# Attention on one core: products with the values in two runs a pair, last 64 rows and keys by full 128x128 transposes

## The chip, the core and the metric

The kernel runs on one core of a Trainium2 chip. The metric is the device time of one execution in microseconds (us). Engines are named as in the profile: PE is TensorE (matmuls), PEld its weight loads, DVE is VectorE, ACT is ScalarE, POOL is GpSimd, SP issues most of the DMAs.

## What is computed

The reference is an attention with a relative position bias, then a mixture of experts, then a maximum of three products. Only the attention is touched by the change (cut to what matters):

```python
B, H, S, D = 4, 8, 576, 64
scores = scale * q @ k.T                 # per batch and head, 576 x 576
scores = scores + bias                   # one 576 x 576 table per head
attn = exp(scores - max(scores))
attn = attn / (sum(attn) + 1e-9)
x = attn @ v                             # per batch and head, 576 x 64
```

576 is four times 128 and a rest of 64 rows (the tail), both of queries and of keys.

## The kernel before, in words

Heads are taken two at a time: there are 16 pairs (four batches, four pairs each). A pair is five steps, numbered 0 to 4 (`it`). Steps 0 to 3 take 128 queries of both heads, step 4 the last 64 queries of both heads in one tile of 128 partitions. The loop over all 80 steps (L488) is written out by hand, and every engine works its instructions in that program order. PE does in one step, in this order:

1. the scores of the step (`scores`, L253), one PSUM tile of two banks for a head, tag S with two buffers;
2. in the part called `mid` (L323): the normalization of the step before is issued to DVE and POOL (`norm_step`, L350), then one item of preparation for the next pair (`prep`, L172: transposes of queries, keys or the tail), then, in six of the sixteen pairs, one item of row work of the batch that is done (`row_q`: logits, or transposes of finished rows);
3. the products with the values (`av`, L398) that the table AV (L473) names for this step;
4. the transposes of the normalized attention of two steps before (`transpose_step`, L368).

DVE adds the bias and takes the maximum for a head (L268), then forms the low part of the prepared item (L199 to L207), then copies the transposed attention of head 0 (L382). ACT first copies the prepared item (`split`, L182), then takes the exponentials (L280), then copies the output of a finished query half (`evict_o`, L411: DVE for half 0, ACT for half 1), then the transposed attention of head 1 (L382) and its 64 last keys (L391).

All transposes (`pt`, `tp`, `tq`, the row tiles `xr_p`) share one PSUM tag T with three buffers, in rotation: the fourth tile waits until the first has been read by everybody.

The output of a pair, `oT`, is made for queries 0 to 255 (half 0, `pT0`, 256 columns) and 256 to 575 (half 1, `pT1`, 320 columns). For keys in chunks 0 to 3 the weights are 128x64 for each head, the two heads write the two halves of the PSUM partitions, and the profile shows them as tiles of 128*64. Chunk 4 (the last 64 keys of both heads together) is one full product of 128*128. In float32 the compiler makes two instructions of each product. Which chunks go where is one table:

```python
PREP0 = ("tail", "k", "q", None, None)
PREP = ("tail", None, "k", "q", None)
AV = (((1, 0, (2, 3)),), ((1, 0, (4,)),), ((1, 1, (0, 1)),), ((1, 1, (2, 3, 4)),), ((0, 0, (0, 1)),))
```

An entry of AV is (pair before or this one, half, chunks). So a pair has four runs of 128*64 products: steps 0, 2, 3 and 4. PREP says what is prepared for the next pair in which step. The prepared queries are moved to other partitions by DMAs from SP (L216, L220) right after DVE has made their low part; step 0 of the next pair needs them. The load of the same item for the pair after the next is issued in the same step (L525).

The tail's queries and keys are loaded to 64 partitions and turned by two transposes of 64x128 (L176). The last 64 queries' last 64 keys are turned by one product of 64*64 for each head (L395).

Of the kernel before, what the change touches and what calls it, by code (L numbers as in the profile page):

```python
# [12 lines left out]
F32 = mybir.dt.float32  # L13
# [4 lines left out]
ALU = mybir.AluOpType  # L18
# [4 lines left out]
P = 128  # L23
B, H, S, D = 4, 8, 576, 64
# [14 lines left out]
TAIL = S - 4 * P  # L39
# [57 lines left out]
def attention(tc, A, ident, x_dram, route, rpool, store):  # L97
    nc = tc.nc
    with ExitStack() as ctx:
# [4 lines left out]
        pl = ctx.enter_context(tc.tile_pool(name="pl", bufs=2, reuse_waits="tile"))  # L104
# [16 lines left out]
        HALF = (slice(0, D), slice(D, P))  # L121

        def load_pair(b, hp):

            t = {}
            for nm in ("q", "k"):
                t[nm] = pl.tile([P, 4, 2, D], F32, name=f"{nm}n", tag=f"{nm}n", bufs=1)
            t["tail"] = pl.tile([TAIL, 2, 2, D], F32, name="tn", tag="tn", bufs=1)
            t["v"] = pl.tile([P, 4, 2, D], F32, name="vn", tag="vn")


            t["qz"], t["vt"] = qz[hp % 2], vd[hp % 2]
            t["qs"] = pl.tile([P, 2, 512], F32R, name="qs", tag="qs")
            t["qd"] = qd[hp % 2]
            t["kh"] = pl.tile([P, 2, S], F32R, name="kh", tag="kh")
            t["kn"] = pl.tile([P, S], F32R, name="kn", tag="kn2")
            t["kl"] = pl.tile([P, S], F32R, name="kl", tag="kl")

            def load(nm):
                hs = slice(2 * hp, 2 * hp + 2)  # L140
                if nm == "tail":
                    for i, x in enumerate(("q", "k")):
                        nc.sync.dma_start(out=t[nm][:, i], in_=A[x][b, hs, 4 * P :].rearrange("h p d -> p h d"))
                    return
                for h in range(2):
                    nc.sync.dma_start(out=t[nm][:, :, h, :], in_=A[nm][b, 2 * hp + h, : 4 * P].rearrange("(c p) d -> p c d", p=P))
                if nm == "v":
                    for h in range(2):
                        nc.sync.dma_start(out=t["vt"][HALF[h], h, :], in_=A["v"][b, 2 * hp + h, 4 * P :])

            t["load"] = load
            return t

        st = [load_pair(*pairs[0])]
        mod = route.modality_rows()

# [15 lines left out]
        def prep(t, nm, pt):  # L172

            if nm == "tail":
                for i in range(2):
                    nc.tensor.transpose(pt[:, i * TAIL : (i + 1) * TAIL], t["tail"][:, i].rearrange("p h d -> p (h d)"), ident[:TAIL, :TAIL])  # L176
            else:
                for c in range(4):
                    nc.tensor.transpose(pt[:, c * P : (c + 1) * P], t[nm][:, c, :, :].rearrange("p h d -> p (h d)"), ident)
            return pt  # L180
# [130 lines left out]
        pTt = pb.tile([P, S], F32, name="pTt", bufs=1)  # L311
# [38 lines left out]
        def norm_step(mz, es):  # L350
            n = len(es)
            nc.vector.tensor_scalar(mz[:, 1, :n], mz[:, 1, :n], 1e-9, None, op0=ALU.add)
            nc.vector.reciprocal(mz[:, 1, :n], mz[:, 1, :n])
            pr = pb.tile([P, 2 * S], F32, name="pr", tag="pr", bufs=2)
            nc.gpsimd.tensor_scalar(pr[:, :S], es[0], mz[:, 1, 0:1], 1.0, op0=ALU.mult, op1=ALU.mult)  # L355
            if n == 2:
                r = mz[:, 1, 1:2]
                nc.gpsimd.tensor_scalar(pr[:, S : S + TAIL], es[1][:, 4 * P :], r, 1.0, op0=ALU.mult, op1=ALU.mult)
                nc.gpsimd.tensor_scalar(pr[:, S + TAIL :], es[1][:, : 4 * P], r, 1.0, op0=ALU.mult, op1=ALU.mult)
            return pr  # L360

        def ptile(t, h, it):
            if it < 2:
                return t["pT0"][:, h, :, it * P : (it + 1) * P]
            q = it * P - Q0
            return t["pT1"][:, h, :, q : q + (P if it < 4 else TAIL)]

        def transpose_step(t, it, pr):  # L368
            if it == 0:
                t["pT0"] = pb.tile([P, 2, 4, Q0], F32, name="pT0", tag="pT0", bufs=1)  # L370
                t["pTt"] = pTt
            if it == 2:
                t["pT1"] = pb.tile([P, 2, 4, Q1], F32, name="pT1", tag="pT1", bufs=1)
            for h in range(2):
                if it == 4 and h == 1:
                    break
                o = 0 if h == 0 else S + TAIL
                tp = ps.tile([P, 512], F32, name="tp", tag="T", bufs=3)
                for c in range(4):
                    nc.tensor.transpose(tp[:, c * P : (c + 1) * P], pr[:, o + c * P : o + (c + 1) * P], ident)  # L380
                if it < 4:
                    (nc.scalar.copy if h else nc.vector.tensor_copy)(ptile(t, h, it), tp.rearrange("p (c q) -> p c q", c=4))  # L382
                else:
                    for j in range(2):
                        (nc.scalar.copy if j else nc.vector.tensor_copy)(
                            ptile(t, j, it), tp.rearrange("p (c h q) -> p c h q", c=4, h=2)[:, :, j, :]
                        )
            tq = ps.tile([P, 512], F32, name="tq", tag="T", bufs=3)
            if it < 4:
                nc.tensor.transpose(tq[:, :P], pr[:, 4 * P : 4 * P + P], ident)  # L390
                nc.scalar.copy(t["pTt"][:, it * P : (it + 1) * P], tq[:, :P])  # L391
            else:
                for h in range(2):
                    hs = slice(h * D, h * D + D)
                    nc.tensor.matmul(tq[hs, :TAIL], pr[hs, 4 * P : S], ident[hs, hs], start=True, stop=True)  # L395
                nc.vector.tensor_copy(t["pTt"][:, 4 * P :], tq[:, :TAIL])

        def av(t, j, cs):  # L398
            if cs[0] == 0:
# [68 lines left out]
            todo = [lambda: lt.append(logits_t(b, xTs, alloc)), last_logits]  # L468
            return todo + [lambda r=r: rows(b, r, xTs, r % 2 or b == B - 1, alloc, row) for r in range(5)]

        PREP0 = ("tail", "k", "q", None, None)
        PREP = ("tail", None, "k", "q", None)
        AV = (((1, 0, (2, 3)),), ((1, 0, (4,)),), ((1, 1, (0, 1)),), ((1, 1, (2, 3, 4)),), ((0, 0, (0, 1)),))  # L473
        st = st + [None] * len(pairs)
        ROWS = (1, 2, 3, 4)
        LR = 4
# [11 lines left out]
        for i in range(len(steps) + 5):  # L488
            n, it = i // 5, i % 5
            cur = st[n] if n < len(pairs) else None  # L490
            last = st[n - 1] if n > 0 else None
            if cur:
                nm = (PREP if n else PREP0)[it]
                nxt = (st[n + 1], nm) if n + 1 < len(pairs) and nm else None
                mid = row_q and it in ROWS
                soft, pr = soft_step(cur, pairs[n][1], it, nxt, pend, row_q.pop(0) if mid else None, n >= len(pairs) - NP2, early.pop(0) if early else None)
            else:
                soft, pr = None, norm_step(*pend) if pend else None
            ready[i - 1] = pr
            pend = soft  # L500
            for back, j, cs in AV[it]:
                t = last if back else cur
                if t:
                    av(t, j, cs)
                    if 4 in cs:
                        evict_o(t, j)
            if 0 <= i - 2 < len(steps):
                m, jt = steps[i - 2]
                transpose_step(st[m], jt, ready.pop(i - 2))
            for f in EARLY.get((n, it), ()):  # L510
                f()
            if last and it == 3:
                b, hp = pairs[n - 1]
                if hp == NP2 - 1:
                    xTs = [st[n - NP2 + i2]["xT"] for i2 in range(NP2)]
                    if b == B - 1:
                        assert not ops
                        return lambda *allocs: batch_done(b, xTs, *allocs)
                    row_q += batch_done(b, xTs, talloc, lambda: px.tile([P, DM], F32, name="xr", tag="xr"))
            if n < len(pairs):  # L520
                if it == 0 and n + 2 < len(pairs):
                    st[n + 2] = load_pair(*pairs[n + 2])
                if it == 4 and n + 1 < len(pairs):
                    st[n + 1]["load"]("v")
                if nm and n + 2 < len(pairs):  # L525
                    st[n + 2]["load"](nm)
            if i > 7:
                next(gates, None)
            if i > 4:
                next(rconst, None)  # L530
# [1003 lines left out]
```

## Time and profile before

| | us |
|---|---|
| median of three runs (lowest to highest) | 961.23 (958.93 to 961.49) |
| profiled execution: device time | 962.84 |
| profiled execution: span, first to last instruction | 961.1 |
| PE busy | 930.1 |
| DVE busy | 549.8 |
| ACT busy | 429.9 |
| POOL busy | 219.0 |

The mean granted TensorE clock of the profiled execution is 0.995 of full speed. The span goes from the first to the last instruction; the device time has 1.7 us more around it. The steps of the attention with their scores run from 51.60 us to 363 us of the span; the last products with the values end at 370 us. Ahead of them lies the making of the bias table, behind them the experts and the three products.

To read a timeline row: start, length until the last of the group ends, engine, line, operation, tiles written and read, TensorE tile, shapes, count; in brackets the idle time before it and what ended it. Neighbouring instructions of one kind are merged to one row. A matmul's length has its way through the array in it, so the pace is read from starts and not from lengths.

### The profile page before, as it was taken

What the parts mean: (1) busy time and instruction counts of PE and PEld (TensorE: products, weight loads), DVE (VectorE), ACT (ScalarE), POOL (GpSimd) and SP (SyncE); (2) the same over time, 40 slices, a digit from 0 to 9 for tenths busy, and PEclk for the clock granted to TensorE, in tenths of its full rate; (3) what the DMA queues carried; (4) which work ended last, traced back from release to release, by engine and by line L of the source; (5) the groups of instructions that cost most, each with busy time, mean ns of one, the idle gap of its engine ahead of it and who ended that gap; (6) DMA issues with size and microseconds to landing.
All of it is one profiled execution on the core that took longest, in us unless ns stands there. A gap on an engine that the chain in (4) does not pass through costs nothing. (4 is left out here: it accounts for less than half of the span.)

```text
span 961.1 us, 16962 instructions
## 1 busy us (share of the span) xinstructions
PE 930.1 (97%) x5667; PEld 727.7 (76%) x5667; DVE 549.8 (57%) x1262; ACT 429.9 (45%) x889; POOL 219.0 (23%) x355
## 2 busy tenths in 40 slices
PE   6989999999999998999999999999999999999996
PEld 3437777777777776788888887888888888888885
DVE  7966777877877887533344368525455365522221
ACT  6977766766767665322244256433111011112222
POOL 1004544353363446211111111110000000001111
PEclk9999999999999999999999999999999999999999
DMA  5976664764565563312244469405021131001111
GB/s 123 211 186 170 144 142 100 179 146 103 145 158 128 132 182 127 107 45 59 64 130 135 143 183 327 140 33 164 1 88 45 43 89 44 22 12 44 44 44 55
DMA packets 111036, 106.67 MB, mean 111 GB/s; under 512 B 69787, under 2 KB 79259, under 8 KB 110940
## 3 DMA queue, kind: packets, MB, share of 16 engines
q1 hardware_dynamic: 106140, 90.53, 34.7%
q0 software_dynamic: 4800, 14.97, 5.1%
q8 instruction: 47, 0.77, 0.4%
q14 instruction: 49, 0.40, 0.1%
HBM read 121.57 MB, written 14.96 MB: 142 GB/s over the span
## 5 line engine op out<-in xcount | busy, mean ns | idle before, releaser
L280 ACT ACTIVATE e<-e,mz 128x576 f32<-128x576 f32 x144 | 110.6, 770 | 35.2 <-DVE mz L268 35.1
L1288 PE MATMUL acc<-x2h,w3h 128*128 128x512 f32 x288 | 114.7, 398 | 0.0
L1288 PE MATMUL acc<-x2l,w3h 128*128 128x512 f32 x288 | 113.8, 395 | 0.0
L1288 PE MATMUL acc<-x2h,w3l 128*128 128x512 f32 x288 | 113.7, 395 | 0.0
L268 DVE CUSTOM_DVE_ANT_0 e<-s,bias 128x576 f32<-128x576 f32 x140 | 101.6, 756 | 20.3 <-PE s L262 18.9
L355 POOL TENSOR_SCALAR pr<-e,mz 128x576 f32<-128x576 f32 x80 | 59.7, 746 | 222.0 <-DMA bias<-ev 74.5
L1294 DVE TENSOR_TENSOR h<-acc,h 128x512 f32<-128x512 f32 (+1 forms) x60 | 38.2, 636 | 102.1 <-PE acc L1288 101.8
L380 PEld LDWEIGHTS tp<-ident,pr 128*128 128x128 f32 x576 | 64.6, 142 | 26.6 <-issue 10.8
L925 DVE TENSOR_TENSOR hl<-ht,hh 128x512 fp32r<-128x512 f32 x42 | 29.1, 692 | 95.8 <-ACT hh L924 86.7
L1317 POOL DMA_INDIRECT out_dram<-res,tok x18 | 17.3, 959 | 289.4 <-ACT res L1316 289.4
L380 PE MATMUL tp<-ident,pr 128*128 128x128 f32 x576 | 79.7, 279 | 1.1 <-POOL pr L355 0.8
L409 PE MATMUL oT<-pT,vn 128*64 128x320 f32 (+1 forms) x512 | 76.7, 418 | 0.0
L1288 PEld LDWEIGHTS acc<-x2h,w3l 128*128 128x128 f32 x288 | 54.3, 189 | 12.5
L1314 PE MATMUL op<-woh,hs 128*128 128x512 f32 x204 | 63.5, 389 | 0.0
L1288 PEld LDWEIGHTS acc<-x2l,w3h 128*128 128x128 f32 x288 | 54.3, 189 | 11.9
L1288 PEld LDWEIGHTS acc<-x2h,w3h 128*128 128x128 f32 x288 | 54.3, 189 | 11.9
L382 DVE COPY pT<-tp 128x512 f32<-128x512 f32 x64 | 44.2, 690 | 33.2 <-PE tp L380 32.7
L1419 PE MATMUL bp<-gt,w2d 128*32 128x512 f32 (+1 forms) x512 | 51.9, 429 | 9.5 <-ACT w2d L1405 7.4
L1292 ACT COPY h<-acc 128x512 f32<-128x512 f32 (+1 forms) x30 | 16.3, 544 | 99.2 <-PE acc L1288 99.1
L262 PE MATMUL s<-kh,qs 128*128 128x288 f32 x248 | 59.4, 321 | 1.1 <-DMA qs<-hl 1.1
L987 POOL DMA_INDIRECT y_dram<-y,sca x21 | 21.5, 1026 | 161.3 <-ACT hh L924 145.6
L262 PE MATMUL s<-kl,qz 128*128 128x288 f32 x248 | 53.7, 298 | 1.3 <-DMA qz<-hl 1.1
(294 smaller groups left out, 2059.5 us busy)
## 6 DMA issues: line engine op xcount, KB each, us to landing
store<-in_moe_w_dram SPq DMA_DIRECT2D x160, 512.0 KB
bias<-ev SPq DMA_DIRECT2D x32, 288.0 KB
kh<-kn SPq DMA_DIRECT2D x64, 144.0 KB
raw<-in_moe_w_dram SPq DMA_DIRECT2D x18, 512.0 KB
qs<-hl SPq DMA_DIRECT2D x64, 128.0 KB
xr<-y_dram SPq DMA_DIRECT2D x18, 256.5 KB
kn<-in_k_dram SPq DMA_DIRECT2D x32, 128.0 KB
qn<-in_q_dram SPq DMA_DIRECT2D x32, 128.0 KB
```

The source lines that it names most:

```text
L262: nc.tensor.matmul(s[:, j, :SH], w, k[:, j * SH : (j + 1) * SH], start=i == 0, stop=i == len(terms) - 1)
L268: nc.vector.tensor_tensor_reduce(out=e.rearrange("p (a j) -> p a j", a=2), in0=s, in1=bt.rearrange("p (a j) -> p a j", a=2), op0=ALU.add, ...
L280: nc.scalar.activation(e, e, AF.Exp, bias=mz[:, 0, h : h + 1], scale=-1.0, accum_out=mz[:, 1, h : h + 1])
L355: nc.gpsimd.tensor_scalar(pr[:, :S], es[0], mz[:, 1, 0:1], 1.0, op0=ALU.mult, op1=ALU.mult)
L380: nc.tensor.transpose(tp[:, c * P : (c + 1) * P], pr[:, o + c * P : o + (c + 1) * P], ident)
L382: (nc.scalar.copy if h else nc.vector.tensor_copy)(ptile(t, h, it), tp.rearrange("p (c q) -> p c q", c=4))
L409: nc.tensor.matmul(oT[hs, :n], vt[:, c, h, :], t[f"pT{j}"][:, h, c, :], start=c == 0, stop=False)
L925: nc.vector.tensor_tensor(out=lo[:, j : j + 512], in0=pt[:, j : j + 512], in1=h[:, j : j + 512].bitcast(F32), op=ALU.subtract)
L1288: nc.tensor.matmul(a[:, :n], wt[:, m, ws], xt[:, c, :], start=c == 0 and k == 0, stop=c == KC - 1 and k == 2)
L1294: nc.vector.tensor_tensor(out=d, in0=a[:, :n], in1=d, op=ALU.max)
L1314: nc.tensor.matmul(o, hs[:, ht, f, :], wt, start=f == 0 and k == 0, stop=f == FC - 1 and k == 2)
L1419: nc.tensor.matmul(out[c0 : c0 + 32, : hi - lo], ws, gs[g][:, lo:hi], start=True, stop=True, tile_position=(0, c0))
```

## The change

The chunks of the products are put together (two runs of 128*64 products a pair, in steps 2 and 4), keys and queries are prepared one step earlier, and the pieces of 64 rows become full transposes. For the last, the tail's keys go to partitions 64 to 127 of the tail's tile, POOL writes the last 64 keys of step 4's attention a second time beside themselves, and DVE copies the two diagonal blocks of the transposed tile.

```diff
-            t["tail"] = pl.tile([TAIL, 2, 2, D], F32, name="tn", tag="tn", bufs=1)
+            t["tail"] = pl.tile([2 * TAIL, 2, D], F32, name="tn", tag="tn", bufs=1)
...
-                        nc.sync.dma_start(out=t[nm][:, i], in_=A[x][b, hs, 4 * P :].rearrange("h p d -> p h d"))
+                        nc.sync.dma_start(out=t[nm][HALF[i]], in_=A[x][b, hs, 4 * P :].rearrange("h p d -> p h d"))
...
-                for i in range(2):
-                    nc.tensor.transpose(pt[:, i * TAIL : (i + 1) * TAIL], t["tail"][:, i].rearrange("p h d -> p (h d)"), ident[:TAIL, :TAIL])
+                nc.tensor.transpose(pt[:, :P], t["tail"].rearrange("p h d -> p (h d)"), ident)
...
+            if n == 1:
+
+                nc.gpsimd.tensor_scalar(pr[:, S : S + TAIL], es[0][:, 4 * P :], mz[:, 1, 0:1], 1.0, op0=ALU.mult, op1=ALU.mult)
...
+            nc.tensor.transpose(tq[:, :P], pr[:, 4 * P : 4 * P + P], ident)
             if it < 4:
-                nc.tensor.transpose(tq[:, :P], pr[:, 4 * P : 4 * P + P], ident)
                 nc.scalar.copy(t["pTt"][:, it * P : (it + 1) * P], tq[:, :P])
             else:
                 for h in range(2):
                     hs = slice(h * D, h * D + D)
-                    nc.tensor.matmul(tq[hs, :TAIL], pr[hs, 4 * P : S], ident[hs, hs], start=True, stop=True)
-                nc.vector.tensor_copy(t["pTt"][:, 4 * P :], tq[:, :TAIL])
+                    nc.vector.tensor_copy(t["pTt"][hs, 4 * P :], tq[hs, hs])
...
-        PREP0 = ("tail", "k", "q", None, None)
-        PREP = ("tail", None, "k", "q", None)
-        AV = (((1, 0, (2, 3)),), ((1, 0, (4,)),), ((1, 1, (0, 1)),), ((1, 1, (2, 3, 4)),), ((0, 0, (0, 1)),))
+        PREP = ("tail", "k", "q", None, None)
+        AV = (((1, 0, (4,)),), (), ((1, 1, (0, 1, 2, 3)),), ((1, 1, (4,)),), ((0, 0, (0, 1, 2, 3)),))
...
-                nm = (PREP if n else PREP0)[it]
+                nm = PREP[it]
```

## Rows read from the trace of the kernel before

**Rows 1.** Page, busy time: us (share of the span) x instructions.

```profile
PE 930.1 (97%) x5667; PEld 727.7 (76%) x5667; DVE 549.8 (57%) x1262; ACT 429.9 (45%) x889; POOL 219.0 (23%) x355
```

**Rows 2.** Timeline of one pair without row work, PE: start us, length us, ...

```profile
104.59 0.52 PE L262 MATMUL s<-kh,qs 128*128 128x288 f32 x2
...
105.82 0.34 PE L176 MATMUL pt<-ident,tn 64*128 64x64 f32 x2
106.09 1.08 PE L409 MATMUL oT<-pT,vn 128*64 128x256 f32 x8
...
107.10 1.09 PE L380 MATMUL tp<-ident,pr 128*128 128x128 f32 x8
...
108.06 0.51 PE L262 MATMUL s<-kh,qs 128*128 128x288 f32 x2
...
109.20 0.59 PE L405 MATMUL oT<-pTt,vd 128*128 128x256 f32 x2
...
109.63 0.60 PE L380 MATMUL tp<-ident,pr 128*128 128x128 f32 x4
...
110.16 0.33 PE L395 MATMUL tq<-ident,pr 64*64 64x64 f32 x4
...
110.42 0.53 PE L262 MATMUL s<-kh,qs 128*128 128x288 f32 x2
...
114.29 0.51 PE L262 MATMUL s<-kh,qs 128*128 128x288 f32 x2
...
115.43 0.60 PE L179 MATMUL pt<-ident,qn 128*128 128x128 f32 x4
...
115.96 1.30 PE L409 MATMUL oT<-pT,vn 128*64 128x320 f32 x8
...
117.18 0.81 PE L405 MATMUL oT<-pTt,vd 128*128 128x320 f32 x2
...
117.83 1.04 PE L380 MATMUL tp<-ident,pr 128*128 128x128 f32 x8
...
118.73 0.77 PE L262 MATMUL s<-kn,qd 128*128 128x288 f32 x4
```

**Rows 3.** Timeline, PE: first and last of five steps 0 that lasted longer.

```profile
121.67 0.52 PE L262 MATMUL s<-kh,qs 128*128 128x288 f32 x2
...
125.95 0.51 PE L262 MATMUL s<-kh,qs 128*128 128x288 f32 x2
...
271.04 0.51 PE L262 MATMUL s<-kh,qs 128*128 128x288 f32 x2
...
275.35 0.52 PE L262 MATMUL s<-kh,qs 128*128 128x288 f32 x2
```

**Rows 4.** Groups by form, whole span: x count | busy us, mean ns | idle before.

```profile
L390 PE MATMUL tq<-ident,pr 128*128 128x128 f32 x64 | 17.9, 280 | 2.2 <-DVE xr L449 1.2 <-DVE hl L207 0.9
```

**Rows 5.** Timeline of step 0 of the same pair, DVE.

```profile
105.51 0.76 DVE L268 CUSTOM_DVE_ANT_0 e<-s,bias 128x576 f32<-128x576 f32 x1 [0.23 <-PE s L262]
...
106.89 0.46 DVE L199 SCALAR_TENSOR_TENSOR qd<-pt,qd 64x64 fp32r<-64x64 f32 x2
...
107.37 0.23 DVE L202 TENSOR_TENSOR kl<-pt,kn 128x64 fp32r<-128x64 f32 x1
```

**Rows 6.** Timeline of steps 1 to 3 of the same pair, ACT and POOL.

```profile
109.71 0.31 POOL L358 TENSOR_SCALAR pr<-e,mz 128x64 f32<-128x64 f32 x1
...
111.37 0.35 ACT L385 COPY pT<-tp 128x256 f32<-128x256 f32 x1
...
116.56 0.77 ACT L280 ACTIVATE e<-e,mz 128x576 f32<-128x576 f32 x1
...
117.32 0.76 ACT L280 ACTIVATE e<-e,mz 128x576 f32<-128x576 f32 x1
...
118.08 0.41 ACT L416 COPY xT<-oT 128x320 f32<-128x320 f32 x1
...
118.90 0.59 ACT L382 COPY pT<-tp 128x512 f32<-128x512 f32 x1 [0.42 <-PE tp L380]
```

## The prediction

> **What bounds the kernel now.** I read the page first: PE is busy 97% of the span, the next engine, DVE, 57% [rows 1]. That says PE sets the pace, but a busy PE may be a PE that drains. So I read PE's timeline of one pair without row work next, by starts. Its five steps last 3.47, 2.36, 3.87, 4.44 us [rows 2] and 2.94 (118.73 to 121.67) [rows 2, 3], together 17.08. In this pair PE waits for nobody; what can be saved are the places where the form of the tile changes. The third view is the timeline of DVE and ACT in the same steps: it tells how late their copies come, and so which wait ends last when PE gets faster.
>
> **PE's saving, step by step.** Pace at full tiles: two products of 256 columns in 0.43 (109.20 to 109.63), so 0.215 each and by columns 0.27 for 320; eight `tp` and the `tq` in 0.90 (117.83 to 118.73); the scores of a step 1.14 (114.29 to 115.43) [rows 2]. Two tiles of 128*64 run side by side, so a run of eight is four slots.
> - Step 0: from the end of the scores (105.73) to 108.06 are 2.33. Without changes of form: one tail transpose 0.11, four slots 0.86, nine transposes 0.90, together 1.87. Saved: 0.46.
> - Step 1: from 109.63 to 110.42 are 0.79 for four transposes and the small `tq` [rows 2]; five full ones are 0.47. Saved: 0.32.
> - Step 3: from 115.43 to 118.73 are 3.30 [rows 2]; four preparations 0.43, four slots 1.08, two products 0.54 and 0.90 are 2.95. Saved: 0.35.
> - Steps 2 and 4 keep their run, twice as long; nothing is saved there.
>
> That is 1.1 a pair, some 17.8 us over 16 pairs if nothing else came of it, and PE alone would need 15.95 a pair: 2.58, 2.04, 4.95, 2.58 and 3.80 in steps 0 to 4.
>
> Here the Trainium skill speaks against the change: TensorEngine Tiling, section Theoretical Speedup, gives tiles of at most 64 rows up to twice the speed. By that rule the small transposes cost no more than the full ones and an estimated 0.26 (tail) and 0.3 (`tq`) a pair of the saving would be missing. The trace disagrees: the small forms, with the change into them, took 0.27 and 0.26 before the next work started [rows 2].
>
> **What is late next.** The work of DVE and ACT stays, and their order in a step is fixed. Steps 0, 1 and 3 get short, so PE arrives earlier at tiles that others have yet to read or write.
> - Step 0, the buffers of tag T: `tq` is the fourth tile after the tail's, so it waits until DVE has made the tail's low part. DVE begins on the scores 0.92 after the step starts and ends the low part at 107.60, 3.01 after [rows 2, 5]. PE would be at `tq` after 2.55. New wait: 0.5. That PE does wait in this way shows in the idle time before `tq`, 0.9 of it ended by DVE's low part of the queries [rows 4].
> - Step 2: the run now needs, ahead of its first chunks as before, the two half copies of step 4's attention, of which ACT makes one in step 1, after both exponentials. Step 1 now prepares the keys, as step 3 prepared the queries before; there the exponentials started 2.27 and 3.03 after the step's start and the next copy at 3.79 [rows 2, 6]. So the half copy (0.35 [rows 6]) ends 4.2 after step 1 started, 2.1 into step 2. PE is there after 1.14 + 0.43 + 0.1 = 1.7. New wait: 0.5.
> - Step 4: the run of all four chunks needs ACT's copy of head 1 from step 3. In step 3 the exponentials now start at 0.92 + 0.76 + 0.1 = 1.8 and 2.55 and end at 3.3 [rows 5, 6]; then come the output's copy, 0.41, and the copy itself, 0.59 [rows 6]: 4.3 after the step's start. PE is there at 2.58 + 0.95 (six score products and the change of form) = 3.55. New wait: 0.75. Before, step 3 lasted 4.44 and the copy was hidden.
>
> So 1.75 of new waits against 1.1 saved: a pair gets longer by 0.6. Nine pairs are of this kind: +5.4. In six pairs row transposes on PE give the copies more time, but row tiles also take T buffers and copies; between -0.5 and +1.0 each I take +0.3, since half of their steps are as above: +1.8. The first pair has only a part: +0.2.
>
> **The DMAs.** Five steps 0 lasted longer than 3.47 because PE waited for the moved queries: the first by 0.81 (4.28), the last by 0.84 (4.31) [rows 3], the five together by 4.0. Preparing the queries one step earlier issues all ten moves of that item, and on SP the load that follows them, some 4 us earlier, the length of the step between; the longest of these waits was 1.35. They go: -4.0. The key moves and the loads keep their distance of one pair to their use; bounds for them 0 and +1.
>
> **Small terms.** POOL writes 64 columns more once a pair, 0.31 [rows 6]; the reader comes a step later and POOL is busy 23% [rows 1], so nothing; without that cover 16 x 0.31 = 5.0. DVE makes two copies instead of one in step 1, some 0.2 that falls into the step 2 wait. After the last scores nothing competes: -0.4 from the changes of form there.
>
> **Sum**: 5.4 + 1.8 + 0.2 - 4.0 - 0.4 = +3.0. Against the profiled execution's own 962.84 that is 965.8; that execution stands 1.6 above the median of 961.23, so for a median I say 964.2. A measurement of this kernel can tell 0.3%, 2.9 us, from no change; the forecast lies on the edge of it, on the slower side.
>
> **Rivals.**
> 1. *Not slower: the copies are in time.* Place: the waits ahead of the runs in steps 2 and 4 and of `tq` in step 0. For it: ACT is busy 45%, DVE 57% [rows 1], and a wait in one step lets the copies catch up for the next. Against it: the starts in rows 5 and 6 leave little. The waits decide below 1.4 a pair (16 x 0.3 = 4.4, what the DMAs and the end give), and below 1.2 the kernel is faster by over 0.3%. At half my waits, 0.88: 16 x (0.88 - 1.1) - 4.4, about 953; with no waits 939. Chance 0.26.
> 2. *No change:* the waits at 1.2 to 1.55 a pair cancel savings and DMAs: 961. Every wait here is a difference of two times known to 0.1 or 0.2, so this is close to the forecast. Chance 0.34.
> 3. *The forecast:* waits of 1.6 to 1.9, DMA waits gone. 964.2, chance 0.28.
> 4. *The DMA waits stay* because what delays the moves is SP's queue and not DVE: 4.0 more, 968. Against it: the moves stand right behind DVE's low part. Chance 0.09.
> 5. *The small tiles were free*, the rule above: the 0.56 a pair isn't saved, 16 x 0.56 = 9, so 973. The trace speaks against it. Chance 0.03.
>
> Faster therefore 0.26, same 0.34, slower 0.28 + 0.09 + 0.03 = 0.40. The range of 8 in 10 goes from rival 1 at half my waits, 953, to 0.6 on all sixteen pairs with the DMA waits kept, 971.
>
> **What would show it.** In PE's timeline a quiet pair of about 3.1, 2.0, 5.4, 2.6 and 4.6 between the starts of the scores; idle time before `tq` in step 0 ended by DVE's low part (L202), before the run in step 2 by ACT's half copy, before the run in step 4 by ACT's copy of head 1; no idle time of the scores ended by a DMA; two weight-load gaps for changes of form a pair instead of four, and none at the tail and `tq`. Steps 0 to 4 near 2.6, 2.0, 4.95, 2.6, 3.8 would prove me wrong and rival 1 right; a step 0 that still waits for `qs` or `qz` rival 4.

## The result: 0.8% slower, and where the time stands

The changed kernel takes 968.94 us (median of six runs, 967.86 to 969.63), the kernel before 961.36 on the same chips (958.93 to 962.35): ratio 1.0082 [1.0067, 1.0097]. The profiled execution of after took 967.86 with a span of 966.1 and a mean granted clock of 0.993; that of before took 962.84 [rows 1 and the table above]. So between the two profiled executions there are +5.0, between the medians +7.6: the one profiled lies 1.5 above its median and the other 1.1 below. What follows tells where the +5.0 are; no trace shows the other 2.6.

The page's busy times of after (us, share of the span, instructions) hardly differ from [rows 1]:

```profile
PE 924.5 (96%) x5603; PEld 733.2 (76%) x5603; DVE 550.5 (57%) x1278; ACT 428.4 (44%) x889; POOL 225.6 (23%) x371
```

PE is busy 5.6 less, as the missing small forms would have it, and the kernel is longer. So the time is in waits. First the timeline of PE for a pair without row work, the counterpart of [rows 2] (start, length, engine, line, ...; idle time and what ended it in brackets):

```profile
104.63 0.51 PE L261 MATMUL s<-kh,qs 128*128 128x288 f32 x2
...
106.31 1.04 PE L382 MATMUL tp<-ident,pr 128*128 128x128 f32 x8
107.74 0.30 PE L391 MATMUL tq<-ident,pr 128*128 128x128 f32 x1 [0.39 <-DVE kl L201]
107.80 0.51 PE L261 MATMUL s<-kh,qs 128*128 128x288 f32 x2
...
109.84 0.52 PE L261 MATMUL s<-kh,qs 128*128 128x288 f32 x2
...
111.53 2.83 PE L410 MATMUL oT<-pT,vn 128*64 128x320 f32 x16
114.29 1.09 PE L382 MATMUL tp<-ident,pr 128*128 128x128 f32 x8
...
115.25 0.51 PE L261 MATMUL s<-kh,qs 128*128 128x288 f32 x2
...
117.83 0.77 PE L261 MATMUL s<-kn,qd 128*128 128x288 f32 x4
...
118.96 2.43 PE L410 MATMUL oT<-pT,vn 128*64 128x256 f32 x16
121.32 1.09 PE L382 MATMUL tp<-ident,pr 128*128 128x128 f32 x8
...
122.28 0.51 PE L261 MATMUL s<-kh,qs 128*128 128x288 f32 x2
```

From one start of the scores to the next the steps are 3.17, 2.04, 5.41, 2.58, 4.45, together 17.65; before they were 3.47, 2.36, 3.87, 4.44, 2.94, together 17.08. Steps 0, 1 and 3 won 2.5, steps 2 and 4 lost 3.05.

Two stretches of the timeline with all engines tell why (same columns), in step 2 and in step 4:

```profile
111.59 0.36 ACT L387 COPY pT<-tp 128x256 f32<-128x256 f32 x1
...
111.99 1.81 PEld L410 LDWEIGHTS oT<-pT,vn 128*64 128x64 f32 x14 [0.28 <-ACT pT L387]
...
118.51 0.40 ACT L417 COPY xT<-oT 128x320 f32<-128x320 f32 x1
...
118.81 0.58 ACT L384 COPY pT<-tp 128x512 f32<-128x512 f32 x1
118.96 0.19 PEld L410 LDWEIGHTS oT<-pT,vn 128*64 128x64 f32 x2 [0.33 <-ACT xT L417]
...
119.45 1.49 PEld L410 LDWEIGHTS oT<-pT,vn 128*64 128x64 f32 x14 [0.29 <-ACT pT L384]
```

In both steps PE has begun its run and stops after its first product (head 0 of the first chunk), until ACT has made head 1's copy, which stands in its queue behind two exponentials. In step 4 the run also begins late: `oT` has one buffer, and the first weight load waits for ACT's output copy (L417), which stands behind the same exponentials (0.33 of idle time, where e5, with that copy on DVE, has 0.17). Over the whole attention the groups of waits say the same (us in total, times, longest):

```profile
PE tq L391 <- DVE kl L201: 3.2, 8, 0.4
...
PEld oT L410 <- ACT pT L387: 2.7, 10, 0.3
PEld oT L410 <- ACT xT L417: 2.7, 8, 0.3
...
PEld oT L410 <- ACT pT L384: 2.4, 8, 0.3
```

No group of after in that stretch has scores that wait for a DMA; all five long steps 0 [rows 3] are 3.17 now.

**The balance.** I take the stretch from the scores of step 3 of the first pair to the first product of the experts (L934). It is 289.06 before (80.94 to 370.00) and 294.13 after (79.55 to 373.68), +5.07; what lies ahead is 1.4 shorter, what lies behind 1.3 longer.

| part | forecast | measured |
|---|---|---|
| five waits for DMAs | -4.0 | -4.0 |
| five quiet pairs (1, 2, 3, 7, 11), without those waits | +3.0 | +2.9 |
| three pairs with logits in step 4 (4, 8, 12), likewise | +1.8 | +0.2 |
| six pairs with row work | +1.8 | +4.5 |
| first pair | +0.2 | +0.9 |
| last pair and what follows it | +0.2 | +0.7 |

(Pairs are counted from 0. The last row is the quiet pair 15, +0.6, and -0.4 for the end in the forecast.) The parts that were read from a timeline came out; those that were taken from a neighbour did not.

### The profile page after: what moved, and what is told of

It is laid out like the page before. It is cut to its first block, busy times and chain, and to the rows that moved or that the text cites. A ratio compares the mean times of both kernels' runs of the same rounds, so it can differ in the third digit from the quotient of the medians.

```text
span 966.1 us, 16904 instructions
## 1 busy us (share of the span) xinstructions
PE 924.5 (96%) x5603; PEld 733.2 (76%) x5603; DVE 550.5 (57%) x1278; ACT 428.4 (44%) x889; POOL 225.6 (23%) x371
## 5 line engine op out<-in xcount | busy, mean ns | idle before, releaser
L382 PE MATMUL tp<-ident,pr 128*128 128x128 f32 x576 | 78.6, 277 | 2.1 <-POOL pr L354 0.8
L410 PEld LDWEIGHTS oT<-pT,vn 128*64 128x64 f32 x512 | 41.4, 136 | 26.3 <-ACT pT L387 2.7
```

The source lines that it names most:

```text
L410: nc.tensor.matmul(oT[hs, :n], vt[:, c, h, :], t[f"pT{j}"][:, h, c, :], start=c == 0, stop=False)
```

## Experiments

Steps are lengths in a pair without row work and without a wait for a DMA, from starts of the scores in one profiled execution; the stretch is the one above. Each stretch is from one execution, whose time stands in the column "profiled". That execution can lie off its kernel's median: before's is 1.5 above, e7's 4.1 below. So steps and stretches tell what that execution did, and medians and ratios decide whether a kernel is faster.

One thing in the stretches does not go with the edits. In step 3 of the first pair TensorE was granted a clock of 0.5, the lower of its two levels (1.2 of 2.4 GHz), for 3.4 us in the traces of before, after, e3, e6, e7 and e11, and full clock in the other eight. The first pair is the same in before and e4; its steps 3 and 4 take 6.58 at the low clock (before) and 5.89 at the full one (e4). So between a kernel of the one group and one of the other some 0.7 of the stretch is the clock, an estimate from these two. What set it low the traces do not show: PE's idle times ahead of it are alike, 0.80, 0.30 and 0.90 in before, 0.81, 0.30 and 0.90 in e1.

| kernel | steps 0 to 4 | pair | stretch | profiled | median | ratio to before |
|---|---|---|---|---|---|---|
| before | 3.47 2.36 3.87 4.44 2.94 | 17.08 | 289.06 | 962.84 | | |
| after | 3.17 2.04 5.41 2.58 4.45 | 17.65 | 294.13 | 967.86 | 968.94 | 1.0082 [1.0067, 1.0097] |
| e1 full transposes alone | 3.32 2.03 4.00 4.44 2.94 | 16.73 | 285.30 | 959.43 | 960.51 | 0.9994 [0.9980, 1.0009] |
| e2 and early preparation | 3.31 2.47 4.25 4.00 2.94 | 16.99 | 286.90 | 963.18 | 961.69 | 1.0006 [0.9991, 1.0021] |
| e3 two runs alone | 3.20 1.93 5.08 3.24 4.33 | 17.78 | 294.27 | 966.77 | 967.76 | 1.0078 [1.0061, 1.0095] |
| e4 early preparation alone | 3.47 2.80 3.88 4.00 2.94 | 17.09 | 286.28 | 960.59 | 960.15 | 0.9986 [0.9972, 1.0001] |
| e5 after, output copied by DVE | 3.17 2.04 5.42 2.57 4.12 | 17.32 | 291.39 | 964.21 | 964.74 | 1.0039 [1.0023, 1.0055] |
| e6 after, half copies by DVE | 3.17 2.05 5.02 2.57 4.45 | 17.26 | 290.91 | 962.88 | 964.55 | 1.0035 [1.0018, 1.0051] |
| e7 after, run in step 0 | 4.18 2.48 4.99 2.58 2.20 | 16.42 | 283.62 | 956.59 | 960.67 | 0.9986 [0.9970, 1.0003] |
| e8 e7 and e5 | 4.18 2.48 4.99 2.58 1.88 | 16.09 | 284.20 | 957.40 | 959.46 | 0.9972 [0.9954, 0.9990] |
| e9 e8, loads later | as e8 | 16.09 | 282.62 | 954.95 | 955.71 | 0.9945 [0.9929, 0.9962] |
| e10 e9, rows in step 0 | 4.18 2.48 4.99 2.57 1.88 | 16.10 | 277.62 | 951.65 | 952.25 | 0.9917 [0.9888, 0.9946] |
| e11 e10, small forms | 4.34 2.80 4.96 2.57 1.88 | 16.55 | 282.82 | 954.58 | 955.01 | 0.9930 [0.9906, 0.9953] |
| e12 e10, three runs | 3.58 3.68 4.93 2.58 1.88 | 16.65 | 281.57 | 955.04 | 955.67 | 0.9928 [0.9899, 0.9956] |

### The three parts, apart

**e1**: the changed kernel with the old order of preparation and the old products; the full transposes stay. The diff is against the changed kernel.

```diff
-        PREP = ("tail", "k", "q", None, None)
-        AV = (((1, 0, (4,)),), (), ((1, 1, (0, 1, 2, 3)),), ((1, 1, (4,)),), ((0, 0, (0, 1, 2, 3)),))
+        PREP0 = ("tail", "k", "q", None, None)
+        PREP = ("tail", None, "k", "q", None)
+        AV = (((1, 0, (2, 3)),), ((1, 0, (4,)),), ((1, 1, (0, 1)),), ((1, 1, (2, 3, 4)),), ((0, 0, (0, 1)),))
...
-                nm = PREP[it]
+                nm = (PREP if n else PREP0)[it]
```

> Only the full transposes; runs and preparation as before. Theory A (the long runs bring the new waits, the full transposes are pure saving): step 1 of a quiet pair 2.05 instead of 2.36, step 0 3.3 instead of 3.47 (the 0.26 saved at the tail is partly taken by the wait of tq for DVE's low part), a quiet pair 16.5 to 16.6, the five DMA waits stay; total 6 to 8 us under before, about 954. Rival B (full transposes with one more POOL write and one more DVE copy cost what they save, or are themselves what made the changed kernel slower): same as before or up to 7 us more, 961 to 969.

Measured: a pair of 16.73. Step 0 gives 0.15, step 1 0.33, and step 2 takes 0.13 back, so 0.35 a pair in place of some 0.5. The five waits for the moved queries stay and spread, as steps 0 of 3.56 to 4.74, and step 2 of row pair 5 goes from 5.05 to 5.42. The six row pairs gain nothing: 115.3 together, as before. The stretch is 3.8 shorter, some 0.7 of that by the clock. The median is only 0.8 lower, which is no difference, where 6 to 8 were expected, so this missed. The profiled executions differ by 3.4 (962.84 and 959.43); that the medians differ by less is that the one lies 1.5 above its median and the other 1.1 below. That the full transposes save PE's time shows in the quiet pair alone, here and in e11.

**e2**: e1 with the new order of preparation, which is the changed kernel with the old products; the diff is against the changed kernel.

```diff
-        AV = (((1, 0, (4,)),), (), ((1, 1, (0, 1, 2, 3)),), ((1, 1, (4,)),), ((0, 0, (0, 1, 2, 3)),))
+        AV = (((1, 0, (2, 3)),), ((1, 0, (4,)),), ((1, 1, (0, 1)),), ((1, 1, (2, 3, 4)),), ((0, 0, (0, 1)),))
```

> Full transposes and the earlier preparation, the four short runs as before. Theory A: quiet pair 16.7 (3.3, 2.5, 4.0, 4.0, 2.9), no idle time of the scores ended by a DMA in steps 0 (-4.0), some 1.5 to 3.5 us more in the six pairs with row work; total about 953 to 956. Rival C (the earlier preparation is what made the changed kernel slower): over 961.

Measured: 961.69, no gain, so this missed. The waits for DMAs go but for one step 0 of 4.26, and the pair gets longer, 16.99, by the step 2 that now has the query preparation; step 2 of row pair 5 is 6.11. By its number alone this is rival C's case (over 961); e3 and e4 speak against that rival.

**e3**: the kernel before with the new AV and nothing else.

```diff
-        AV = (((1, 0, (2, 3)),), ((1, 0, (4,)),), ((1, 1, (0, 1)),), ((1, 1, (2, 3, 4)),), ((0, 0, (0, 1)),))
+        AV = (((1, 0, (4,)),), (), ((1, 1, (0, 1, 2, 3)),), ((1, 1, (4,)),), ((0, 0, (0, 1, 2, 3)),))
```

> Only the two long runs; preparation and small transposes as before. Theory A: the waits are all there and the preparation of the queries in step 3 adds to the one in step 4: quiet pair 17.9 to 18.0 (3.0 to 3.2, 2.0 to 2.4, 5.3, 3.2, 4.4), DMA waits remain; total 973, 12 us over before. Rival B or C (the loss is in the other parts): the two saved changes of form a pair show, 0.6 x 16 = 10 us less, 951.

Measured: 967.76, less than expected, with the sign of the theory. This part makes the whole loss by itself: its pair of 17.78 stands beside 17.65 for all three parts. Fewer changes of form, and 0.7 a pair longer.

**e4**: the kernel before with the new order of preparation and nothing else.

```diff
-        PREP0 = ("tail", "k", "q", None, None)
-        PREP = ("tail", None, "k", "q", None)
+        PREP = ("tail", "k", "q", None, None)
...
-                nm = (PREP if n else PREP0)[it]
+                nm = PREP[it]
```

> Only the earlier preparation. Theory A: the five long steps 0 become 3.47 (-4.0), quiet pairs stay at 17.1 with 0.44 moved from step 3 to step 1, pairs with row work 0 to 0.7 longer; total 958 to 960. Rival C: the preparation in step 1 delays DVE and ACT and costs, total 964 or more. Rival D (the DMA waits come from SP's queue, not from when the queries are ready): steps 0 of 4.3 to 4.8 stay.

Measured: 960.15, beside the 958 to 960 expected and at the edge of what can be told. Every step 0 is 3.47: the five waits of [rows 3] are gone by this edit alone, and the quiet pair is what it was (17.09). The six row pairs take 1.8 more together. Rival 4's forecast fails: moves that are issued a step earlier are in time. What made them late in five pairs of the kernel before is not settled by it, since the earlier issue would cover a held queue as well (e8 shows one).

### The waits of the changed kernel, one at a time

**e5**: the output of half 1 is copied by DVE and not by ACT, so ACT comes 0.40 earlier to the copy for the run in step 4.

```diff
-                (nc.vector.tensor_copy if t is st[len(pairs) - 1] else nc.scalar.copy)(t["xT"][:, Q0:], t["oT"][:, :Q1])
+                nc.vector.tensor_copy(t["xT"][:, Q0:], t["oT"][:, :Q1])
```

> The changed kernel, but the output of query half 1 is copied by DVE instead of ACT in step 3. Theory A (step 4's long run waits for ACT, which makes the output's copy and then head 1's copy behind two exponentials): ACT reaches head 1's copy 0.35 to 0.4 earlier, step 4 goes from 4.45 to 4.1, a quiet pair from 17.65 to 17.3; total 4 to 6 us under the changed kernel, 963 to 965. Rival E (the long run itself is slower, not late): step 4 stays 4.45 and the total 969.

Measured: 964.74 and a step 4 of 4.12. The timeline of its step 4, PE and ACT:

```profile
117.11 0.77 PE L261 MATMUL s<-kn,qd 128*128 128x288 f32 x4
...
118.08 2.26 PE L410 MATMUL oT<-pT,vn 128*64 128x256 f32 x16
120.27 1.09 PE L382 MATMUL tp<-ident,pr 128*128 128x128 f32 x8
...
117.79 0.56 ACT L384 COPY pT<-tp 128x512 f32<-128x512 f32 x1
```

From the step's start to the transposes after the run it takes 3.16, in after 3.49 (117.83 to 121.32). So ACT's queue is what the run waits for, at its start and for head 1's copy. Some of it is left: the run takes 2.19 to the transposes (118.08 to 120.27), in e10 1.88, and ACT's copy of head 1 still ends 0.27 after the run has begun (117.79 + 0.56 = 118.35).

**e6**: both half copies of step 4's attention by DVE.

```diff
-                        (nc.scalar.copy if j else nc.vector.tensor_copy)(
+                        nc.vector.tensor_copy(
```

> The changed kernel, but both half copies of step 4's attention (made in step 1) are made by DVE. Theory A (step 2's long run waits for ACT's half copy behind two exponentials): step 2 from 5.41 to about 5.2, step 4 unchanged; in the pairs with row work DVE has more to do and step 2 of the first of them gets 0.2 to 0.3 longer; total 1 to 3 us under the changed kernel. Rival E: step 2 stays 5.41.

Measured: 964.55 and a step 2 of 5.02, more than expected. PE's timeline of its step 2, the run with no stop in it:

```profile
110.20 2.44 PE L410 MATMUL oT<-pT,vn 128*64 128x320 f32 x16
112.57 1.09 PE L382 MATMUL tp<-ident,pr 128*128 128x128 f32 x8
```

The run takes 2.37 to the next transposes; in after it took 2.76 (111.53 to 114.29).

**e7**: the run of half 0 goes from step 4 to the next step 0, where PE waited for DVE, and its chunk 4 to step 1.

```diff
-        AV = (((1, 0, (4,)),), (), ((1, 1, (0, 1, 2, 3)),), ((1, 1, (4,)),), ((0, 0, (0, 1, 2, 3)),))
+        AV = (((1, 0, (0, 1, 2, 3)),), ((1, 0, (4,)),), ((1, 1, (0, 1, 2, 3)),), ((1, 1, (4,)),), ())
```

> The changed kernel, but the long run of query half 0 is put a step later, into step 0 of the next pair (its chunk 4 into step 1), where the copies it reads are a step old. Theory A: the waits ahead of it and of tq in step 0 go; steps of a quiet pair 4.2, 2.5, 5.0, 2.6, 2.2, sum 16.4; DMA waits gone; total 15 to 18 us under the changed kernel, about 952, and 9 under the kernel before. Rival E: a quiet pair stays at 17.6, 969. Rival B (the full transposes bring what is lost): a gain of 2 to 4 us at the most.

Measured: the quiet steps as expected, 16.42 a pair. Still two runs, the same products, and 1.23 a pair less: this is what the waits in steps 0, 2 and 4 cost, all but what is left in step 4 (2.20, of which e8 takes 0.32). The sum was missed: 960.67 and not 952. The profiled execution took 956.59, so its trace shows some 4.6 of that miss and not the other 4.1. Pair 11 has a step 0 of 5.88, 1.5 of it a wait of the scores for the moved queries, and row pairs lose. In step 2 of row pair 5 PE stands before the row transposes:

```profile
161.85 0.66 PE L446 MATMUL xr_p<-ident,xT 128*128 128x128 f32 x4 [0.73 <-ACT pT L387]
```

The row tile is the fourth in tag T after a tile that ACT has yet to copy: the same rule as for `tq` in step 0, in another place.

### What the shorter steps wait for

**e8**: e7 and e5 together, so both edits shown above.

> As the run in step 0, and the output of half 1 copied by DVE. Theory A: step 4 another 0.35 shorter (1.8 instead of 2.2), quiet pair 16.1; total 3 us under the run in step 0, about 949. Rival: DVE is the next bound there (its work of a pair is some 15.5 with row work more), then the same as the run in step 0.

Measured: the quiet pair exactly as expected, 16.09. The total was not, 959.46 and not 949: long steps 0 came back, of 5.47, 5.04, 4.80 and 5.43. SP's timeline ahead of the second of them, and PE's weight loads of its scores (SPq is SP's queue; length is that of the issue):

```profile
111.03 2.56 SPq L146 DMA_DIRECT2D kn<-in_k_dram  x2
...
114.24 1.11 SPq L215 DMA_DIRECT2D qs<-hl  x2
...
117.33 0.59 SPq L219 DMA_DIRECT2D qz<-hl  x1
...
119.67 0.30 PEld L261 LDWEIGHTS s<-kl,qz 128*128 128x128 f32 x2 [0.34 <-DMA qz<-hl]
```

The scores of this step 0 come 1.9 after those of step 4 (116.15 to 118.03), in after 4.45: the moves have lost that much slack. And the load of raw keys that stands ahead of them took SP 2.56; in after the same load took 1.15.

**e9**: e8, and the loads for the pair after the next are issued two steps later, behind the moves.

```diff
-                if nm and n + 2 < len(pairs):
-                    st[n + 2]["load"](nm)
+                if it >= 2 and n + 2 < len(pairs):
+                    st[n + 2]["load"](PREP[it - 2])
```

> The run in step 0 with DVE's output copy, and the loads for the pair after the next issued two steps later, so that on SP no load stands between the key moves and the query moves. Theory F (the long steps 0 of 4.8 to 5.5 that came back with the run in step 0 are SP's queue: a load holds it 2.6 us ahead of the query moves): all steps 0 after the first pairs 4.2, some 3 us less than without the later loads; about 956. Rival G (the moves land late for another reason, or the loads only shift the wait to another step): long steps 0 stay, total unchanged, 959 to 960.

Measured: 955.71, as expected in total, and only in part for the reason given. No scores wait for a moved query any more, yet steps 0 of pairs 1, 3 and 11 last 4.87, 4.85 and 5.71. In all three PE waits for the raw tail (0.50, 0.48 and 1.34), which the edit loads later: the edit's own price. SP's and PE's timeline at pair 3:

```profile
110.95 2.52 SPq L215 DMA_DIRECT2D qs<-hl  x2
...
119.12 0.30 PE L175 MATMUL pt<-ident,tn 128*128 128x128 f32 x1 [0.48 <-DMA tn<-in_k_dram]
```

The raw tail comes too late for its transpose. The long issue did not go with the load: now the first move after the key moves has it, 2.52.

**e10**: e9, with the row work in steps 0, 1, 3 and 4 and none in step 2.

```diff
-        ROWS = (1, 2, 3, 4)
+        ROWS = (0, 1, 3, 4)
```

> As the later loads, and row work in steps 0, 1, 3 and 4 instead of 1 to 4, so that the step with the long run and the query preparation has none. Theory H (in the six pairs with row work step 2 is long, 6.5 instead of 5.0, since the row tile waits for a T buffer that ACT's half copy holds): first row pair from 20.9 to about 19.6, second from 17.7 to 17.3, together 3 to 4 us less than with the later loads alone; about 953. Rival: PE's work is only moved, each row tile costs its 0.43 wherever it stands, no gain.

Measured: 952.25, as expected (the intervals of the ratios of e9 and e10 overlap). The six row pairs take 114.9 together, in e9 118.5; step 2 of pair 5 goes from 6.52 to 5.11. (The late tail is still there: steps 0 of pairs 1, 3 and 4 last 4.94, 4.75 and 4.63.) This is the best version: 9.0 less than the kernel before on the same chip (ratio 0.9917 [0.9888, 0.9946]), and some 17 less than the changed one. Its quiet pair on PE:

```profile
101.84 0.51 PE L261 MATMUL s<-kh,qs 128*128 128x288 f32 x2
...
103.19 1.95 PE L410 MATMUL oT<-pT,vn 128*64 128x256 f32 x16
105.07 1.09 PE L382 MATMUL tp<-ident,pr 128*128 128x128 f32 x8
106.00 0.27 PE L391 MATMUL tq<-ident,pr 128*128 128x128 f32 x1
...
108.03 0.60 PE L382 MATMUL tp<-ident,pr 128*128 128x128 f32 x4
...
108.50 0.51 PE L261 MATMUL s<-kh,qs 128*128 128x288 f32 x2
```

The run of half 0 (103.19 to 105.07, 1.88) now fills the time in which DVE makes the tail's low part, and `tq` waits for nobody.

### What a change of form costs

**e11**: e10 with the small transposes of the kernel before (tail and last 64 keys), their loads and their copies.

```diff
...
-                nc.tensor.transpose(pt[:, :P], t["tail"].rearrange("p h d -> p (h d)"), ident)
+                for i in range(2):
+                    nc.tensor.transpose(pt[:, i * TAIL : (i + 1) * TAIL], t["tail"][:, i].rearrange("p h d -> p (h d)"), ident[:TAIL, :TAIL])
...
-                    nc.vector.tensor_copy(t["pTt"][hs, 4 * P :], tq[hs, hs])
+                    nc.tensor.matmul(tq[hs, :TAIL], pr[hs, 4 * P : S], ident[hs, hs], start=True, stop=True)
...
```

> The kernel of the row work in steps 0, 1, 3 and 4, with the small transposes of 64 rows back. There the quiet pairs wait for nobody, so PE's own price of the small forms shows. Theory A: step 0 0.25 longer, step 1 0.3 longer, a quiet pair 16.6 to 16.65 instead of 16.09; total 8 to 9 us more, about 961. Rival 5 of the prediction (tiles of 64 rows run side by side and cost no more): step times unchanged, 952; where DVE's second copy and POOL's extra write count, a little under 952.

Measured: 955.01 and a pair of 16.55. PE's timeline at the two places:

```profile
102.84 0.33 PE L176 MATMUL pt<-ident,tn 64*128 64x64 f32 x2
103.10 1.95 PE L409 MATMUL oT<-pT,vn 128*64 128x256 f32 x16
...
107.95 0.60 PE L380 MATMUL tp<-ident,pr 128*128 128x128 f32 x4
108.48 0.33 PE L395 MATMUL tq<-ident,pr 64*64 64x64 f32 x4
108.74 0.53 PE L262 MATMUL s<-kh,qs 128*128 128x288 f32 x2
```

Four `tp` and `tq` take 0.79 (107.95 to 108.74) against 0.47 in e10 (108.03 to 108.50): 0.32. The tail makes step 0 longer by 0.16. PE waits for nothing of note in either kernel there, so this is PE's own price of the small forms, 0.45 a pair. In the total it does not show: 8 to 9 us more were expected, the medians differ by 2.8, and the intervals of the two ratios overlap. The stretch is 5.2 longer, some 0.7 of it by the clock, and the late tails of e10 (steps 0 of pairs 1, 3 and 4) are not there in e11, where these steps are 4.33.

**e12**: e10 with half 0 in two runs, so three a pair.

```diff
-        AV = (((1, 0, (0, 1, 2, 3)),), ((1, 0, (4,)),), ((1, 1, (0, 1, 2, 3)),), ((1, 1, (4,)),), ())
+        AV = (((1, 0, (0, 1)),), ((1, 0, (2, 3, 4)),), ((1, 1, (0, 1, 2, 3)),), ((1, 1, (4,)),), ())
```

> The same kernel with the run of step 0 cut in two: chunks 0 and 1 in step 0, chunks 2 and 3 with chunk 4 in step 1. One run more a pair where nothing waits, so the price of a change of form shows by itself. Theory A: step 0 3.75, step 1 3.25, a quiet pair 16.4 (0.30 to 0.35 more); total 5 us more, about 957. Rival E (the change of form costs nothing, the gaps are only where PE would have waited anyway): a quiet pair 16.1, 952.

Measured: 955.67; the pair is 16.50 to 16.65, so 0.4 to 0.55 for one more run. PE's timeline:

```profile
102.98 1.09 PE L382 MATMUL tp<-ident,pr 128*128 128x128 f32 x8
104.13 0.30 PE L391 MATMUL tq<-ident,pr 128*128 128x128 f32 x1
...
105.33 0.60 PE L178 MATMUL pt<-ident,kn 128*128 128x128 f32 x4
105.86 1.08 PE L410 MATMUL oT<-pT,vn 128*64 128x256 f32 x8
106.87 0.70 PE L406 MATMUL oT<-pTt,vd 128*128 128x256 f32 x2
107.41 0.60 PE L382 MATMUL tp<-ident,pr 128*128 128x128 f32 x4
```

Four preparations and a run of four slots are 0.43 + 0.86; they took 1.54 (105.33 to 106.87), so 0.25 went into the two changes of form, and the full product behind them took 0.54 where e10's took 0.43. The rest is a wait: `tq` comes 1.15 after the transposes' start, in e10 0.93, since the shorter run covers DVE less.

## Why the prediction was right, and what its sum missed

**Sign, range and mechanism held.** It was a little slower, for the reason forecast: PE saved nearly what it should, and the copies of ACT and DVE took the place of the changes of form. The size was too low, +3.0 against +7.6 between the medians. In part the sign was luck: the pairs that were counted as quiet, with the end, gave 2.9 + 0.2 + 0.7 = +3.8 against the -4.0 of the DMAs, and what made the kernel slower were the row pairs, +4.5, of which the forecast had +1.8. And the total lies beside the number of rival 4 (968), whose waits are not there.

**PE's saving, 1.1 a pair.** Right within 0.15. PE alone was put at 15.95; e10's quiet pair, in which nothing of note is waited for, needs 16.10, so the saving is 0.98. The term that was off is the tail's: 0.26 forecast, 0.16 in e11. For `tq` it was 0.30 and 0.32. Rival 5, by which the small forms were free, falls with e11. It drew on the Trainium skill, TensorEngine Tiling (Array Packing), section Theoretical Speedup. The Trainium skill, TensorEngine Tiling (Array Packing), section Key Properties, says that a change of tiling mode drains the engine; the traces of e11 and e12 agree, where changes of form cost time in steps without a wait. In e12 the price was some 0.25 for a run of four slots, in and out together.

**The new waits, 1.75 a pair.** Measured: 17.65 of after less 16.10 of e10, 1.55. That is 0.2 under the forecast and at the upper end of rival 2, no change; since the saving was 0.15 under its forecast too, the difference of the two came out nearer than either. By place: step 0 is 3.17 (forecast 3.1), and its wait ends with DVE's low part of the tail's keys, as it should; step 2 is 5.41 against 4.99 without the wait, 0.42 (forecast 0.5), shown by e6; in step 4 the forecast was 0.75, measured are 4.45 less 3.80, 0.65, and e5 shows 0.33 of it as ACT's output copy. A part of this the forecast did not have: it named head 1's copy alone and not the one buffer of `oT`, for which the run's start waits. What is left in e5, some 0.3, was not taken away by itself; the end of ACT's copy of head 1 there fits it, and e7 shows that it goes when the run moves. A quiet pair is longer by 0.57, forecast 0.6.

**The DMAs, -4.0.** Right, and by the step named: e4 removes all five waits with the order of preparation alone. (The queries' item has six moves, four of `qs` and two of `qz`, and not ten.)

**What failed is the carrying over to pairs that I had not read.**
- *Row pairs, "+0.3 each".* They cost 0.75 each on average, 4.5 in all, inside the bounds of -0.5 and +1.0; pairs 6 and 10 by themselves are above them, 1.1. The step said that row transposes give the copies more time; it named the T buffers as the other side and gave them too little weight. In after the row tiles make PE wait at both ends. The timeline in step 2 of row pair 5 and in step 1 of pair 6:

```profile
166.92 0.66 PE L446 MATMUL xr_p<-ident,xT 128*128 128x128 f32 x4 [0.40 <-ACT pT L387]
...
184.37 0.69 DVE L204 TENSOR_TENSOR kl<-pt,kn 128x512 fp32r<-128x512 f32 x1
...
185.20 0.30 PE L391 MATMUL tq<-ident,pr 128*128 128x128 f32 x1 [0.83 <-DVE gate L650]
```

  The first lengthens a step 2 that went from 5.05 to 6.18, the second a step 1 that went from 2.80 to 3.50 where quiet ones got shorter by 0.32. In the second the row tile makes `tq` the fourth tile in tag T, counted from the prepared keys, and it starts behind DVE's low part of them (184.37 + 0.69 = 185.06); the router's `gate`, which the row names, is DVE's next instruction. That the place of the row work decides is shown by e10, which gets 3.6 back from e9 in the six pairs by moving one item.
- *First pair, "+0.2".* Its step 4 got the long run (3.11 to 3.91) and it has no run in step 3 to lose: +0.9.
- *The end, "-0.4".* The last step 4 has the long run too, and its wait. PE's timeline of it in after:

```profile
364.04 2.43 PE L410 MATMUL oT<-pT,vn 128*64 128x256 f32 x16
...
369.44 0.63 PE L382 MATMUL tp<-ident,pr 128*128 128x128 f32 x4 [0.33 <-DVE pT L384]
```

  From the last scores (362.91) to L934 it takes 10.77, before 9.91. In the sum this pair was a quiet one, though it prepares nothing and has less to save.
- *Pairs with logits.* I counted them as quiet. In their step 4 the logits stand ahead of the run and give ACT its time (the run of pair 4 takes 1.88 to the transposes, as long as in e10): step 4 goes from 4.05 to 5.06, +1.0 in place of +1.5, and the pair costs 0.07. This is the cover that I had credited to the row pairs.

Together +9.1 and not +7.0 beside the DMAs' -4.0. The other 2.6 between profiled executions and medians stay open. Such amounts occur in parts that no edit here touches: in the fourteen traces what lies ahead of the stretch takes 78.6 to 80.9, and what lies behind it 590.3 to 593.7.

## What to carry to other kernels

Where two short runs become one long one, look at what the long run needs at its start: a run that had half its inputs from an earlier step now waits for the last copy of all. The gain was in the edit, but in another place: the same two runs, one of them in a step in which PE waited anyway, with the copies and the queue put right, made 0.9917 out of 1.0082. And make the sum from a timeline of every kind of iteration (quiet, with side work, first, last), since a delta of the quiet one doesn't carry over.

## What was not expected of the hardware

The issue of two DMAs on SP's queue took 1.15 in after, but 2.56 in e8 at the same place of the program, and in e9, where that load was moved away, the move that now followed the four key moves took 2.52. So the hold-up does not go with that load. Nor does it go with the place behind the key moves: between 60 and 370 us every trace, that of before too, has 6 to 12 single issues of 1.0 to 2.8, where others take 0.4 to 0.6, and they are loads, moves and stores alike. SP's timeline of before (a load of values) and of after (a load of the tail):

```profile
179.04 2.38 SPq L149 DMA_DIRECT2D vd<-in_v_dram  x2
...
180.71 1.55 SPq L143 DMA_DIRECT2D tn<-in_k_dram  x1
```

Most of them stand 14 to 19 us or a multiple of that apart. What holds the queue there no run settles. Which instruction is hit differs from trace to trace, and with it which transfer comes late.

A tail transposed in two pieces of 64x128 cost 0.16 more than one full transpose, two products of 64*64 for `tq` 0.32.
